# Grouping the attention products of a chunk by kind: all four pairs of heads at once

## The chip, the cores and the metric

The kernel runs on one core of a Trainium2 chip. The metric is the device time of one execution in microseconds. Before the change three runs took 1051.94, 1056.81 and 1057.1 us, with a median of 1056.81.

## The reference

A gated linear attention (4 sequences, 8 heads, 768 tokens, head size 48) is followed by two MLPs over 3072 tokens of 384 columns:

```python
for t in range(S):
    state = alpha[:, :, t, :, None] * state + einsum('bhd,bhde' outer product of k[t], v[t])
    y[:, :, t] = einsum('bhd,bhde->bhe', q[:, :, t], state)
...
h = x @ w_in;   x1 = (h * sigmoid(h)) @ w_out                    # 384 -> 2048 -> 384
out = (silu(x1 @ w_gate) * (x1 @ w_val)) @ w_out2                # 384 -> 1536 -> 384
```

## The kernel before

**Attention.** The tokens of a sequence are cut into 6 chunks of 128; with 4 sequences these are 24 chunks, ordered by chunk and then by sequence, so that chunk n has position c = n // 4 in sequence b = n % 4. The 8 heads are 4 pairs, the two heads of a pair on partitions 0 to 47 and 64 to 111. For each pair g (96 in all) the kernel makes keys times the decays behind them and queries over these (`stage_a1` to `stage_a3`: scans on VectorE, products on POOL and at the start on VectorE). `qkt(g)` makes the scores of both heads on TensorE and moves the keys to tokens on partitions; `causal(g)` masks the scores on VectorE into a tile `pt`; `keys(g)` copies the keys on ScalarE into a tile `kt`.

`pv(g)` is what the change touches. On TensorE it issues for one pair up to three kinds of plain float32 products, each once per head:

- the value product (L449), into the results `y`: 128 tokens deep, 64 columns wide, 128 moving columns. In the first four chunks a second product (L451) adds the values of pair 0 under the other pairs;
- the state product (L456), for c > 0, adds onto `y`: 64 rows deep, 48 wide, 128 moving columns;
- the increment product (L465), for c < 5, into `ds`: 128 deep, 64 wide, 48 moving columns.

The head decides which half of the columns of the array a product uses, and for the state product which half of the rows too. In the trace every float32 product appears as two matmul records, each with a weight load. `chunk_end(n)` copies a finished chunk's `y` out on ScalarE, with the difference to the full float32 on VectorE, and adds `ds` to the state.

**First MLP.** 24 chunks are 7 blocks of 4, 3, 3, 3, 3, 4, 4. For a block, 16 steps each take 9 products `g1` (L559 to L562) and 9 products `g2` (L594 to L597), 512 or 384 columns wide. Its weights come as 64-bit words that VectorE decodes (L47 to L57), during the first block only. **Second MLP.** 6 blocks of 12 steps, `gv` and `og`.

**The order** is written out by hand; every engine works its instructions in the order in which the program issues them. The first four chunks are attention alone: `attn(2)` issues one pair's products with a lag of two pairs, and then the next pair's scores. From then on, each step of the first MLP has two slots, one behind `g1` and one behind `g2`, and `slot` calls `attn` with lag 1: products of the oldest pair, then scores of a new pair if one is due (12 or 16 pairs over 24 of a block's 32 slots). The attention of a block is worked on in the slots of the block before it.

Of the kernel before, what the change touches and what calls it, by code (L numbers as in the profile page):

```python
# [21 lines left out]
C = 128  # L22
# [7 lines left out]
# Columns of the packed attention input: the decays of each pair of heads with a 0 before and behind  # L30
# them, then keys, queries and values.
# [4 lines left out]
# Bounds on the sums of squares of a chunk's scaled keys and queries, and on the squares of the sums  # L36
# of its results, which are finite with them.
# [3 lines left out]
def decode(eng, raw, tmp, step):  # L41
    """One of three steps from float64 words ([128, 2 n] int32) to the float32 with the same leading
    24 bits, in the place of the high words; the last returns those."""
# [20 lines left out]
def general(tc, pk, w1, w2, out):  # L64
    """The same function for inputs outside the range of the chunked form: the recurrence step by
    step over the tokens (a scan per value column), and the two MLPs in plain float32 products."""
# [154 lines left out]
def fast(ctx, tc, pk, w1, w2, out, bad_i):  # L221
    """Chunked attention in division form and both MLPs, float32 products as three float32r passes
    of operands that are split exactly into two parts."""
# [32 lines left out]
    # ---------------------------------------------------------------- attention  # L256
# [10 lines left out]
    # The keys of a pair with tokens on partitions, the columns of its heads at 0 and 64.  # L267
    kts = [ac.tile([128, 2, 64], F32, name=f"kt{i}") for i in range(3)]

    # Held for the first block of tokens only.  # L270
# [33 lines left out]
    # The score operands are made for two pairs of heads at a time.  # L304
# [7 lines left out]
    # Keys times the decays behind them, queries over these, in three steps. A scan starts anew with  # L312
    # data1 where its factor is 0, between the pairs.
# [11 lines left out]
    def stage_a2(d):  # L325
        n, ps_, _ = duo(d)
        kq_t[d] = ap.tile([128, 2, 2, C], F32, tag="kq", name=f"kq{d}", bufs=4)
        DVE.reciprocal(out=rc_t[d % 2][:, :, 0], in_=r_t[d][:, :, 0])
        KF(d).tensor_tensor(
            out=kq_t[d][:, 0], in0=in_t[n][1][:, 0, ps_], in1=r_t[d][:, :, 1:], op=ALU.mult  # L330
        )
# [40 lines left out]
    def guard(d):  # L372
        """Sums of squares that say at the end whether every product was in range."""
# [9 lines left out]
    def qkt(g):  # L383
        """Scores [key, query] of both heads of a pair, and the keys with tokens on partitions."""
# [3 lines left out]
        if n < NE:  # L388
            # Before the first MLP there is room for a bank per head.
# [15 lines left out]
    def causal(g):  # L405
        if g < NE * NP and g % NP == 0:
            pt = p0[g // NP % 2]
        else:
            pt = ap.tile([128, 2, C], F32, tag="pt", name=f"pt{g}", bufs=3)
# [11 lines left out]
    def keys(g):  # L421
        s = s_t.pop(g)[1]
        if g < (NCH - B) * NP:
            kt_t[g] = kts[g % 3].rearrange("p h x -> p (h x)")
            ACT.activation(
                out=kts[g % 3][:, :, :D], in_=s[:, :2 * D].rearrange("p (h d) -> p h d", h=2),
# [3 lines left out]
    def pv(g):  # L430
        n, p = divmod(g, NP)
        c, b = divmod(n, B)
        v = v_t[n]
        if p == 0:
            early = n % 2 if n < NE else 0
            y_t[n] = bank((6, 2)[early], f"y{n}")
            if c < NC - 1:
                ds_t[n] = bank((7, 3)[early], f"ds{n}")[:, :NP * D].rearrange(
                    "p (r e) -> p r e", r=NP
                )  # L440
        y = y_t[n]
        cs = slice(p * C, p * C + C)
        pt = pt_t.pop(g)
        if n < NE and p == 0:
            p0_t[n] = pt
        else:
            for h in range(2):
                hs = slice(64 * h, 64 * h + 64)
# [544 lines left out]
```

## Time and profile before

| | |
|---|---|
| runs | 1051.94, 1056.81, 1057.1 us |
| profiled execution, span from first to last instruction | 1050.7 us |
| TensorE, matmul | 1017.4 us busy (97%) |
| VectorE | 480.3 us (46%) |
| ScalarE | 366.1 us (35%) |
| POOL | 233.3 us (22%) |

The profiled execution is known by its span; the time around it is in the runs alone. PE is TensorE's matmuls, PEld its weight loads, DVE is VectorE, ACT is ScalarE. PEclk is the granted clock as a share of 2.4 GHz, so 0.5 is the lower level of 1.2 GHz. In a timeline a row merges equal instructions that follow each other (x4): its start is the first one's, its length runs to the end of the last one. Rows of matmuls overlap, since a row lasts until its results are written; the distance between two starts is what a matmul takes from the engine.

### The profile page before, as it was taken

How to read it: one execution, taken by the hardware profiler on the slowest of the kernel's cores; microseconds unless marked ns; L12 is line 12 of the kernel's file. 1: busy time of each engine (PE TensorE's matmuls, PEld its weight loads, DVE VectorE, ACT ScalarE, POOL GpSimd, SP SyncE). 2: the span in 40 equal slices, each digit the busy share in tenths (PEclk: the TensorE clock that was granted, in tenths of full speed). 3: DMA queues.
4: the chain of work that ended last, by engine and by line, in shares of the span. 5: the costliest groups of instructions: out<-in, count | busy, mean ns of one | idle time of the engine just before them, and what ended most of it. 6: DMA issues, size and time to landing. Idle time of an engine off the chain costs nothing.

```text
span 1050.7 us, 14356 instructions
## 1 busy us (share of the span) xinstructions
PE 1017.4 (97%) x5600; PEld 857.1 (82%) x5600; DVE 480.3 (46%) x869; ACT 366.1 (35%) x874; POOL 233.3 (22%) x303
## 2 busy tenths in 40 slices
PE   8888899999999999999999899999999999999997
PEld 5766688898988988877786688888888888888886
DVE  6999954434344354343279983223222222222222
ACT  2444444534444444444344432212212222222211
POOL 5566633313223233231024430000000000000000
PEclk8799999999999999999999999999999999999999
DMA  6544312121112122200155630100100100100000
GB/s 200 207 180 161 116 52 72 51 65 51 52 64 71 48 78 71 78 21 1 36 179 161 187 114 1 61 1 1 61 1 1 61 1 1 61 1 1 31 1 33
DMA packets 27883, 69.09 MB, mean 66 GB/s; under 512 B 3104, under 2 KB 9248, under 8 KB 27808
## 3 DMA queue, kind: packets, MB, share of 16 engines
q1 hardware_dynamic: 27808, 68.10, 20.1%
q8 instruction: 46, 0.75, 0.3%
q14 instruction: 29, 0.24, 0.1%
HBM read 56.68 MB, written 9.44 MB: 63 GB/s over the span
## 4 chain that ended last, share of the span: by engine, by line
PE 79%; DVE 12%; issue 5%; DMA 2%; POOL 1%; ACT 0%; SPq 0%; POOLq 0%; ACTq 0%; DVEq 0%
PE gv L560 9%; PE gv L559 9%; PE gv L562 9%; PE h L559 5%; PE o L664 5%; PE o L662 5%; PE o L663 5%; PE x L594 5%; PE x L595 5%; PE h L560 4%; PE h L562 4%; PE x L597 4%; DVE raw L52 3%; PE y L449 3%; DVE dec L47 2%
## 5 line engine op out<-in xcount | busy, mean ns | idle before, releaser
L560 PE MATMUL gv<-x1h,w 128*128 128x512 f32 x432 | 169.1, 391 | 0.0
L559 PE MATMUL gv<-x1h,w 128*128 128x512 f32 x432 | 169.0, 391 | 0.0
L647 DVE TENSOR_TENSOR a<-gv,sg 128x512 f32<-128x512 f32 x72 | 49.7, 690 | 259.9 <-PE gv L562 258.8
L559 PE MATMUL h<-x,w 128*128 128x384 f32 (+2 forms) x342 | 129.6, 379 | 0.6 <-ACT x L488 0.6
L594 PE MATMUL x<-gh,w 128*128 128x384 f32 (+1 forms) x336 | 122.7, 365 | 4.0 <-ACT gh L578 3.3
L560 PE MATMUL h<-x,w 128*128 128x384 f32 (+2 forms) x342 | 123.2, 361 | 0.0
L562 PE MATMUL gv<-x1l,w 128*128 128x512 f32 x432 | 122.1, 391 | 0.0
L595 PE MATMUL x<-gh,w 128*128 128x384 f32 (+1 forms) x336 | 121.2, 361 | 0.0
L578 ACT ACTIVATE gh<-h 128x384 fp32r<-128x384 f32 (+1 forms) x112 | 59.7, 533 | 167.6 <-PE h L562 167.5
L250 DVE TENSOR_TENSOR gl<-gf,gh 128x384 fp32r<-128x384 f32 (+1 forms) x112 | 72.4, 646 | 80.2 <-ACT gf L579 78.5
L645 ACT ACTIVATE sg<-gv 128x512 f32<-128x512 f32 x72 | 42.9, 596 | 173.3 <-PE gv L562 173.3
L253 ACT ACTIVATE ah<-a 128x512 fp32r<-128x512 f32 x72 | 45.5, 632 | 154.5 <-DVE a L647 154.5
L662 PE MATMUL o<-w,ah 128*128 128x384 f32 x288 | 97.1, 337 | 1.1 <-ACT ah L253 1.1
L664 PE MATMUL o<-w,al 128*128 128x384 f32 x288 | 97.3, 338 | 0.1
L663 PE MATMUL o<-w,ah 128*128 128x384 f32 x288 | 96.7, 336 | 0.0
L250 POOL TENSOR_TENSOR w<-raw,w 128x384 fp32r<-128x384 f32 x64 | 77.6, 1219 | 82.2 <-ACT w L536 78.9
L562 PEld LDWEIGHTS gv<-x1l,w 128*128 128x128 f32 x432 | 81.1, 188 | 17.8
L559 PEld LDWEIGHTS gv<-x1h,w 128*128 128x128 f32 x432 | 81.0, 188 | 15.3
L560 PEld LDWEIGHTS gv<-x1h,w 128*128 128x128 f32 x432 | 81.1, 188 | 15.0
L413 DVE TENSOR_TENSOR pt<-s,mask 128x256 f32<-128x256 f32 x80 | 33.8, 423 | 122.6 <-PE s L402 122.6
L597 PE MATMUL x<-gl,w 128*128 128x384 f32 (+1 forms) x336 | 85.7, 362 | 2.8 <-DVE gl L250 2.5
L562 PE MATMUL h<-x,w 128*128 128x384 f32 (+2 forms) x342 | 85.8, 359 | 0.0
(105 smaller groups left out, 1642.2 us busy)
## 6 DMA issues: line engine op xcount, KB each, us to landing
raw<-in_w_dram SPq DMA_DIRECT2D x64, 384.0 KB, 4.3
in<-in_pk_dram SPq DMA_DIRECT2D x23, 770.5 KB, 4.3
in_v<-in_pk_dram SPq DMA_DIRECT2D x24, 256.0 KB, 3.1
x1r<-x_d SPq DMA_DIRECT2D x6, 768.0 KB, 5.2
out_dram<-ob SPq DMA_DIRECT2D x24, 192.0 KB, 2.0
x_d<-x1e SPq DMA_DIRECT2D x3, 768.0 KB, 4.4
x_d<-x1e SPq DMA_DIRECT2D x4, 576.0 KB, 3.3
late<-in_w_dram SPq DMA_DIRECT2D x4, 384.0 KB, 5.1
```

The source lines that it names most:

```text
L250: eng.tensor_tensor(out=lo, in0=src, in1=hi.bitcast(F32), op=ALU.subtract)
L559: PE.matmul(acc, part(u, k), xh, start=(k == 0), stop=False)
L560: PE.matmul(acc, part(u, k, 1), xh, start=False, stop=False)
L562: PE.matmul(acc, part(u, k), xl, start=False, stop=(k == len(xk) - 1))
L578: ACT.activation(out=gh, in_=hb, func=AF.Silu)
L594: PE.matmul(x1_t[j][m], part(u, m), gh, start=(f == 0), stop=False)
L595: PE.matmul(x1_t[j][m], part(u, m, 1), gh, start=False, stop=False)
L597: PE.matmul(x1_t[j][m], part(u, m), gl, start=False, stop=(f == NF1 - 1))
L647: DVE.tensor_tensor(out=a, in0=val, in1=sg, op=ALU.mult)
L662: PE.matmul(o, ah[:, ts], ohl[:, :DM], start=(f == 0), stop=False)
L663: PE.matmul(o, ah[:, ts], ohl[:, DM:], start=False, stop=False)
L664: PE.matmul(o, al[:, ts], ohl[:, :DM], start=False, stop=(f == NF2 - 1))
```

## The change

`pv` takes a chunk instead of a pair. It issues the value products of all four pairs and both heads, then the increment products of all, then the state products of all. `attn` calls it when all four pairs of a chunk have their scores (and, with lag 2, one pair more); the three other calls of a chunk issue no products. Only the first value product of a chunk starts a new sum in the bank of `y`; the others write into the same bank without a start. To hold four pairs until then, there are 6 buffers of scaled keys and queries instead of 4, 5 masked score tiles instead of 3 and 5 key tiles instead of 3. The reserve for descriptors of dynamic DMAs is set to 4096 bytes. Comments are removed, which moves line numbers by a few (L449 becomes L445, L451 L450, L465 L459, L456 L467).

```diff
-    kts = [ac.tile([128, 2, 64], F32, name=f"kt{i}") for i in range(3)]
+    kts = [ac.tile([128, 2, 64], F32, name=f"kt{i}") for i in range(NP + 1)]
...
-        kq_t[d] = ap.tile([128, 2, 2, C], F32, tag="kq", name=f"kq{d}", bufs=4)
+        kq_t[d] = ap.tile([128, 2, 2, C], F32, tag="kq", name=f"kq{d}", bufs=6)
...
-            pt = ap.tile([128, 2, C], F32, tag="pt", name=f"pt{g}", bufs=3)
+            pt = ap.tile([128, 2, C], F32, tag="pt", name=f"pt{g}", bufs=NP + 1)
...
+    def pv(n):
         c, b = divmod(n, B)
         v = v_t[n]
+        early = n % 2 if n < NE else 0
+        y = y_t[n] = bank((6, 2)[early], f"y{n}")
+        first, last = n * NP, n * NP + NP
+        heads = [(p, h, slice(64 * h, 64 * h + 64)) for p in range(NP) for h in range(2)]
+        pts = [pt_t.pop(g) for g in range(first, last)]
+        for p, h, hs in heads:
+            if n < NE and p == 0:
+                continue
+            cs = slice(p * C, p * C + C)
+            PE.matmul(
+                y[hs, cs], v[:, p, hs], pts[p][:, h], start=(p == (n < NE)),
+                stop=(n >= NE and c == 0 and p == NP - 1),
+            )
+            if n < NE:
                 PE.matmul(
+                    y[hs, cs], v3[n % 2][:, p - 1, hs], pts[0][:, h], start=False,
+                    stop=(p == NP - 1),
                 )
         if c < NC - 1:
+            ds = ds_t[n] = bank((7, 3)[early], f"ds{n}")[:, :NP * D].rearrange(
+                "p (r e) -> p r e", r=NP
+            )
+            for p, h, hs in heads:
+                PE.matmul(
+                    ds[hs, p], kt_t[first + p][:, hs], v[:, p, 64 * h:64 * h + D],
+                    start=True, stop=True,
+                )
...
+        if c:
+            for p, h, hs in heads:
+                PE.matmul(
+                    y[64 * h:64 * h + D, p * C:p * C + C], state[b][hs, p],
+                    kq_t[(first + p) // 2][hs, 1, p % 2], start=False, stop=(p == NP - 1),
+                )
...
-        if st["qk"] - st["pv"] >= lag or not more:
-            if st["pv"] < st["qk"]:
-                pv(st["pv"])
-                st["pv"] += 1
+        if st["qk"] - st["pv"] * NP >= NP + lag - 1:
+            pv(done)
+            st["pv"] += 1
...
-        if st["pv"] > done and done % NP == NP - 1:
-            chunk_end(done // NP)
+        if st["pv"] > done:
+            chunk_end(done)
```

**Order, TensorE, in the slots of the first MLP.** Before, one slot behind `g2` (`x`) with the products of one pair, here the first pair of a chunk of the last sequence (`state_95`), and then the next `g1` (`h`); x2 is both heads:

```order
L597 MATMUL x_1_2_1591<-gl_0_1539,w_1_427 128x384
L449 MATMUL y_1601<-pt_1576,in_v_1166 64x128 x2
L456 MATMUL y_1601<-kq_1069,state_95 48x128 x2
L465 MATMUL ds_1602<-in_v_1166,kt_97 64x48 x2
L559 MATMUL h_2_1609<-x_888,w_4_594 128x384
```

After the change, the slot three steps on, behind the scores of the fourth pair of the same chunk:

```order
L602 MATMUL x_1_2_1595<-gl_3_1664,w_7_694 128x384
L445 MATMUL y_1730<-pt_1580,in_v_1170 64x128 x2
L445 MATMUL y_1730<-pt_1624,in_v_1170 64x128 x2
L445 MATMUL y_1730<-pt_1667,in_v_1170 64x128 x2
L445 MATMUL y_1730<-pt_1708,in_v_1170 64x128 x2
L459 MATMUL ds_1739<-in_v_1170,kt_99 64x48 x2
L459 MATMUL ds_1739<-in_v_1170,kt_100 64x48 x2
L459 MATMUL ds_1739<-in_v_1170,kt_96 64x48 x2
L459 MATMUL ds_1739<-in_v_1170,kt_97 64x48 x2
L467 MATMUL y_1730<-kq_1059,state_95 48x128 x4
L467 MATMUL y_1730<-kq_1210,state_95 48x128 x4
L564 MATMUL h_5_1765<-x_892,w_10_790 128x384
```

The products of three earlier slots have moved into this one, and the state products have moved behind the increments.

**Order, TensorE, in the first four chunks.** Before, around the last products of chunk 1: scores (`s`) of the ninth pair, products of the eighth, scores of the tenth:

```order
L393 MATMUL s_0_337<-kq_258 128x128
L393 MATMUL s_1_338<-kq_258 128x128
L394 MATMUL s_0_337<-start,kq_258 128x96
L449 MATMUL y_286<-pt_315,in_v_111 64x128
L451 MATMUL y_286<-start 64x128
L449 MATMUL y_286<-pt_315,in_v_111 64x128
L451 MATMUL y_286<-start 64x128
L465 MATMUL ds_287<-in_v_111,kt_97 64x48 x2
L393 MATMUL s_5_359<-kq_258 128x128
```

After, the end of the group of chunk 1 and the scores of the tenth pair (four rows each of the two pairs before, between the ninth pair's scores and these, are left out here):

```order
L445 MATMUL y_341<-pt_309,in_v_113 64x128
L450 MATMUL y_341<-start 64x128
L445 MATMUL y_341<-pt_309,in_v_113 64x128
L450 MATMUL y_341<-start 64x128
L459 MATMUL ds_354<-in_v_113,kt_100 64x48 x2
L459 MATMUL ds_354<-in_v_113,kt_96 64x48 x2
L459 MATMUL ds_354<-in_v_113,kt_97 64x48 x2
L459 MATMUL ds_354<-in_v_113,kt_98 64x48 x2
L393 MATMUL s_5_363<-kq_246 128x128
```

Between these two pairs' scores now stands the whole group of the chunk, where the products of one pair stood.

**Order, VectorE, at the end of the first four chunks.** Before, with `x` the eviction of chunk 3 and `raw`, `dec` the decoding of weights:

```order
L47 TENSOR_SCALAR dec_4_536<-raw_4_327 128x384
L250 TENSOR_TENSOR ql<-kq_448,qh 64x2x128
L52 SCALAR_TENSOR_TENSOR raw_4_327<-raw_4_327,dec_4_536 128x384
L47 TENSOR_SCALAR dec_5_560<-raw_5_423 128x384
L57 SCALAR_TENSOR_TENSOR raw_4_327<-raw_4_327 128x384
L250 TENSOR_TENSOR x_276<-y_483,x_276 128x3x128
```

After:

```order
L47 TENSOR_SCALAR dec_4_530<-raw_4_321 128x384
L250 TENSOR_TENSOR ql<-kq_436,qh 64x2x128
L250 TENSOR_TENSOR x_280<-y_546,x_280 128x3x128
L52 SCALAR_TENSOR_TENSOR raw_4_321<-raw_4_321,dec_4_530 128x384
L47 TENSOR_SCALAR dec_5_575<-raw_5_417 128x384
L57 SCALAR_TENSOR_TENSOR raw_4_321<-raw_4_321 128x384
```

The eviction stands three instructions earlier. This is the only difference on VectorE; ScalarE's order is the same, POOL gains two memsets of `kt` at the start, and on SP one load of values stands three weight loads earlier.

## Rows read from the trace of the kernel before

**Rows 1.** The page's totals: busy us, share of the span, instructions.

```profile
PE 1017.4 (97%) x5600; PEld 857.1 (82%) x5600; DVE 480.3 (46%) x869; ACT 366.1 (35%) x874; POOL 233.3 (22%) x303
```

**Rows 2.** Busy us (and instructions) of PE, PEld, DVE, ACT and POOL in stretches of the span, then the granted clock, the DMA share and GB/s.

```profile
0.00:48.00 48.00, 40.40 (x287) 30.15 (x288) 37.52 (x91) 16.93 (x57) 25.82 (x45) 0.79 0.57 189
48.00:134.00 86.00, 71.68 (x406) 52.99 (x406) 83.91 (x132) 39.87 (x102) 57.11 (x56) 0.98 0.45 158
134.00:506.00 372.00, 372.00 (x2401) 315.19 (x2400) 154.06 (x336) 165.91 (x463) 108.10 (x167) 1.00 0.18 55
```

**Rows 3.** Who waited for whom: us in total, times, longest us. The first row is of TensorE from 60 to 505 us, the second of VectorE from 10 to 60 us.

```profile
PE y L449 <- DVE pt L413: 10.7, 10, 1.7
...
DVE pt L419 <- PE s L394: 2.0, 2, 1.0
```

**Rows 4.** Busy us and records of PE and PEld in one stretch, of one line alone: first the state product (L456), then the increment product (L465; its PE count holds two records of another group, its count of weight loads does not).

```profile
134.00:506.00 372.00, 28.71 (x272) 11.38 (x272) 1.00 0.18 55
...
134.00:506.00 372.00, 16.80 (x210) 10.28 (x208) 1.00 0.18 55
```

**Rows 5.** Timeline of TensorE: start us, length us, engine, line, operation, tiles. First a slot of a middle chunk with a pair's products, then, behind the dots, one of a last chunk.

```profile
300.89 0.34 PE L595 MATMUL x<-gh,w 128*128 128x384 f32 x1
...
301.76 0.69 PE L597 MATMUL x<-gl,w 128*128 128x384 f32 x3
302.38 0.44 PE L449 MATMUL y<-pt,in_v 128*64 128x128 f32 x4
302.75 0.42 PE L456 MATMUL y<-kq,state 64*48 64x128 f32 x4
303.10 0.32 PE L465 MATMUL ds<-in_v,kt 128*64 128x48 f32 x4
303.35 0.44 PE L559 MATMUL h<-x,w 128*128 128x384 f32 x1
303.63 0.34 PE L560 MATMUL h<-x,w 128*128 128x384 f32 x1
...
441.26 0.40 PE L560 MATMUL h<-x,w 128*128 128x512 f32 x1
...
442.42 0.86 PE L562 MATMUL h<-x,w 128*128 128x512 f32 x3
...
444.27 0.40 PE L595 MATMUL x<-gh,w 128*128 128x512 f32 x1
```

**Rows 6.** The same view, a pair of an early chunk, where a second value product (L451) follows the first.

```profile
44.02 0.45 PE L449 MATMUL y<-pt,in_v 128*64 128x128 f32 x4
44.29 0.40 PE L451 MATMUL y<-start 128*64 128x128 f32 x4
44.51 0.28 PE L465 MATMUL ds<-in_v,kt 128*64 128x48 f32 x4
44.72 0.44 PE L559 MATMUL h<-x,w 128*128 128x384 f32 x1
```

**Rows 7.** The same view cut to short windows inside the value products of rows 5: weight loads that had begun by 302.50 us, and matmuls that had begun by 302.53 us.

```profile
302.38 0.20 PEld L449 LDWEIGHTS y<-pt,in_v 128*64 128x64 f32 x4 [0.25 <-issue]
...
302.38 0.33 PE L449 MATMUL y<-pt,in_v 128*64 128x128 f32 x2
```

**Rows 8.** Timeline around 133 us, the last pair of chunk 6: VectorE's masking, then TensorE. In brackets the idle time before a row and who ended it.

```profile
132.53 0.42 DVE L413 TENSOR_TENSOR pt<-s,mask 128x256 f32<-128x256 f32 x1
...
133.00 0.44 PE L449 MATMUL y<-pt,in_v 128*64 128x128 f32 x4 [1.03 <-DVE pt L413]
...
133.98 0.50 PE L559 MATMUL h<-x,w 128*128 128x512 f32 x1
```

**Rows 9.** Timelines of the first chunks: POOL's first product behind its memsets, its product for the ninth pair's queries, then TensorE and VectorE at the tenth pair, and TensorE at the lower clock; last, the stretch from 30 to 44 us as in rows 2.

```profile
7.04 0.68 POOL L329 TENSOR_TENSOR kq<-in,r 128x256 f32<-128x256 f32 x1 [1.82 <-DVE r L318]
...
21.64 0.98 POOL L342 TENSOR_TENSOR kq<-in,g 128x256 f32<-128x256 f32 x1 [2.87 <-DVE g L337]
...
24.78 0.49 PE L393 MATMUL s<-kq 64*128 64x128 f32 x4
25.20 0.46 PE L394 MATMUL s<-start,kq 128*128 128x96 f32 x2
...
26.96 0.47 DVE L419 TENSOR_TENSOR pt<-s,mask 128x128 f32<-128x128 f32 x2
...
30.82 0.89 PE L449 MATMUL y<-pt,in_v 128*64 128x128 f32 x4 [1.77 <-DVE pt L419]
31.30 0.83 PE L451 MATMUL y<-start 128*64 128x128 f32 x4
31.73 0.59 PE L465 MATMUL ds<-in_v,kt 128*64 128x48 f32 x4
32.25 0.80 PE L393 MATMUL s<-kq 64*128 64x128 f32 x4
...
30.00:44.00 14.00, 13.07 (x73) 10.81 (x73) 13.25 (x27) 5.07 (x17) 8.68 (x11) 0.51 0.47 162
```

**Rows 10.** Timeline around 301 us: VectorE's masking and its difference, and the product that reads the difference.

```profile
300.92 0.43 DVE L413 TENSOR_TENSOR pt<-s,mask 128x256 f32<-128x256 f32 x1 [3.13 <-PE s L402]
301.38 0.56 DVE L250 TENSOR_TENSOR gl<-gf,gh 128x384 fp32r<-128x384 f32 x1
...
306.53 0.68 PE L597 MATMUL x<-gl,w 128*128 128x384 f32 x3
```

More of the change, by code (lines that the diff above doesn't have):

```diff
@@ L423, in keys @@
         if g < (NCH - B) * NP:
-            kt_t[g] = kts[g % 3].rearrange("p h x -> p (h x)")
+            kt_t[g] = kts[g % (NP + 1)].rearrange("p h x -> p (h x)")
             ACT.activation(
-                out=kts[g % 3][:, :, :D], in_=s[:, :2 * D].rearrange("p (h d) -> p h d", h=2),
+                out=kts[g % (NP + 1)][:, :, :D], in_=s[:, :2 * D].rearrange("p (h d) -> p h d", h=2),
                 func=AF.Copy,
             )
-    def pv(g):
-        n, p = divmod(g, NP)
+    def pv(n):
@@ L432, in pv @@
         c, b = divmod(n, B)
         v = v_t[n]
[L434 to L448, printed above, removed]
-                PE.matmul(y[hs, cs], v[:, p, hs], pt[:, h], start=True, stop=(n >= NE and c == 0))
-                if n < NE:
-                    PE.matmul(
-                        y[hs, cs], v3[n % 2][:, p - 1, hs], p0_t[n][:, h], start=False, stop=True
-                    )
@@ L454, in pv @@
-        if c:
-            for h in range(2):
+        early = n % 2 if n < NE else 0
[12 more added lines that the diff above has]
+            if n < NE:
@@ L456, in pv @@
                 PE.matmul(
-                    y[64 * h:64 * h + D, cs], state[b][64 * h:64 * h + 64, p],
-                    kq_t[g // 2][64 * h:64 * h + 64, 1, g % 2], start=False, stop=True,
+                    y[hs, cs], v3[n % 2][:, p - 1, hs], pts[0][:, h], start=False,
+                    stop=(p == NP - 1),
                 )
         if c < NC - 1:
-            kt = kt_t.pop(g)
-            for h in range(2):
-                hs = slice(64 * h, 64 * h + 64)
-                es = slice(64 * h, 64 * h + D)
-                PE.matmul(ds_t[n][hs, p], kt[:, hs], v[:, p, es], start=True, stop=True)
+            ds = ds_t[n] = bank((7, 3)[early], f"ds{n}")[:, :NP * D].rearrange(
+                "p (r e) -> p r e", r=NP
+            )
@@ new lines, in pv @@
+            for p, h, hs in heads:
[3 more added lines that the diff above has]
+                )
+            for g in range(first, last):
+                kt_t.pop(g)
+        if c:
[4 more added lines that the diff above has]
+                )
@@ L977 @@
     from concourse.bass_utils import run_bass_kernel_spmd
-    nc = bacc.Bacc("TRN2", target_bir_lowering=False, num_devices=1)
+    nc = bacc.Bacc(
+        "TRN2", target_bir_lowering=False, num_devices=1, dynamic_dma_scratch_size=4096
+    )
     arrays, args = {}, []
```

## The prediction

> **What bounds the kernel now.** I read first the page's totals, then the busy time of each engine by stretch, then the waits, and last single slots in the timeline. TensorE is busy 97% of the span, but the stretches show that this average hides three parts [rows 1, 2]. From 0 to 48 us no engine is full: TensorE has 40.40 us and VectorE 37.52, with two waits of about 1.0 us for scores [rows 3]. From 48 to 134 us VectorE is the bound: 83.91 of 86 us busy with weight decoding and scans, while TensorE has 71.68 and waits for it: all ten waits of the value products for masked scores in the attention stretch, 10.7 us, go to this engine [rows 3], and the last one stands just before 133.00 us [rows 8]. From 134 to 506 us TensorE is busy 372.00 of 372 us, VectorE 154.06 and ScalarE 165.91: here, and only here, TensorE time is time of the kernel. After 506 us no attention product is left.
>
> So the question is what the changed products cost TensorE between 134 and 506 us. The counts by line give the amount: 272 records of the state product at 16 for each chunk (4 pairs, 2 heads, 2 records for each float32 product) are 17 chunks, and 208 weight loads of the increment product are 13 chunks [rows 4]. The other four of the 17 are the last chunk of each sequence, which makes no increment. Chunks 4 to 6 are worked on before 134 us, chunks 0 to 3 before 48 us.
>
> **What a pair costs today.** In the timeline of one slot, from the first L597 at 301.76 to the second product of the next group at 303.63 are 1.87 us [rows 5]. Four steps of plain products at 0.174 us (300.89 to 301.76 is five of them) would be 0.70 us. The pair's three kinds therefore cost 1.17 us: 0.10 before L449 starts (301.76 + 3 x 0.174 = 302.28, it starts at 302.38), 0.97 for the three kinds (0.37, 0.35, 0.25), and 0.11 because L559 takes 0.28 to its successor where 0.17 is usual. A chunk pays this four times: 4.69 us. For a chunk without increments, from 442.42 to 444.27 are 1.85 us less four steps of 0.232 (441.26 to 442.42 is five), so 0.92 us, and 3.68 a chunk [rows 5].
>
> What of this is streaming? The early chunks have a place where a second product of the same tile shape follows: L451 behind L449, then L465 behind L451 [rows 6]. There L449 takes 0.27 to its successor, not 0.37, L451 takes 0.22, and L465 with the end of the group 0.21. So 0.22 is the price of two passes of 128 columns for both heads side by side; the first load adds 0.05; and leaving the shape adds 0.10 (0.37 - 0.27). That a load of the next pass runs under the pass before is seen directly: by 302.50 all four loads of the pair had begun, while by 302.53 only two matmuls had [rows 7].
>
> **The change part by part.**
> - *Value products, four pairs in a row:* 0.27 + 3 x 0.22 = 0.93 us. They are followed by increments in the same tile shape, so no 0.10 is paid between them.
> - *Increments:* the first three pairs 0.21 - 0.10 = 0.11 each, the last 0.21 with the way out: 0.54 us.
> - *State products:* their shape (64 rows) never follows itself beyond one pair in this trace. Bounds: 0.22 a pair, as L451 streams the same 128 columns, or 0.35, what a pair costs alone. I take 0.22, since 0.35 holds a first load and a way out, which cannot recur inside a group: 0.35 + 3 x 0.22 = 1.01 us.
> - *Way in and out:* 0.10 and 0.11, once. A chunk costs 0.10 + 0.93 + 0.54 + 1.01 + 0.11 = 2.69 us, so 4.69 - 2.69 = 2.00 us less. Without increments: 0.10 + 0.93 + 0.10 + 1.01 + 0.11 = 2.25, 1.43 less. Sum between 134 and 506 us: 13 x 2.00 + 4 x 1.43 = **31.7 us less**.
> - *Moved work:* in the order shown for the TensorE-bound part, the products of the first three pairs leave their slots and stand with the fourth; the end of a chunk stays in the same slot, so the evictions, state sums and loads behind it hold their places. ScalarE's order does not change, POOL gains two small memsets ahead of its first product, before which it now sits idle for 1.82 us until VectorE is done [rows 9], and that idle time covers them; on SP one load of values moves ahead of three weight loads, which feeds a chunk two further on and costs nothing while VectorE sets the pace.
> - *Hand-over at 133 us:* the last pair of chunk 6 waits for its masked scores (done near 132.95), then takes 0.97 to the next product [rows 8]. In the change the first three pairs' values run under that wait, but the fourth pair's values (0.22 + 0.05), 0.54 of increments and 1.01 of states come behind it: 1.8 us, **0.8 us more**.
> - *The first 48 us:* no product with a state here, but the whole group of a chunk stands between two score products that VectorE reads. For chunk 1 it is 0.27 + 5 x 0.22 + 0.54 = 1.9 us where one pair's 0.70 stands today (44.02 to 44.72 [rows 6]). The scores before it need keys and queries that POOL finishes at 22.62, so they may start near 22.7; with 0.88 for them (24.78 to 25.66), 1.9 and 0.88 again, the next are ready at 26.4, before VectorE's 26.96 [rows 9]. At the lower clock (0.51 from 30 to 44 us, so nearly all at 1.2 GHz) a pair took 0.48 + 0.43 + 0.52 rather than 0.27 + 0.22 + 0.21; the group is then 0.48 + 5 x 0.43 + 3 x 0.22 + 0.52 = 3.8 us and the scores 1.4, and VectorE would wait 2.3 us. Chunk 0 wins up to 1.3 us (one of the waits for scores of about 1.0 goes [rows 3], and up to 0.3 with it) and gives it back behind its group, and some 2 us more at the lower clock. Bounds -1.3 to +4.5 (2.3 + 2.2); I take **0.5 us more**, near the case of the rows at the full clock. The eviction of chunk 3 moves ahead of a decode on VectorE, as the order shows; its products end near 45.6 in the new order and ScalarE's copy near 46.2, when VectorE comes free at 46.1, so it costs 0.1.
> - *Deeper buffers (masked scores, keys, scaled keys and queries):* they only loosen waits; a missing one would show as POOL or ScalarE waiting for TensorE.
>
> What is late next? A slot without products is 1.17 us shorter. The chain that a slot needs: VectorE's difference ends at 301.94, and the L597 that reads it starts at 306.53 [rows 10]. 4.6 us of room less 1.2 leaves 3.4, so nothing new ends last.
>
> Sum: 31.7 - 0.8 - 0.5 = 30.4 us off. The page gives the profiled execution's span, 1050.7 us, and not what lies around it; the three runs lie 1.2 to 6.4 us above the span, their median 1056.81 being 6.1 above. Span after: 1020.3 us; time, with the same 6.1: **1026.4 us**.
>
> **The rivals.**
> 1. *Loads exposed inside a group.* If a load waits for the pass that streams, seven more passes of each kind pay 0.05: 3 x 7 x 0.05 = 1.05 us a chunk, 0.70 without increments, 16.5 us in all; the time would be 1043 us. If only the first load of each further pair did, it would be 3 x 3 x 0.05 = 0.45, 7 us in all, and 1033.4 us. Against it stand the loads that begin under a pass and the 0.22 of L451 [rows 6, 7]; for it, that the 64-row shape is seen only for one pair. This is also what the Trainium skill would make of it ("TensorE: Matmul & The Clock Gate", Part 3, The mechanism): a weight load overlaps with a matmul in flight only when its row group differs, and here every pair of a head has the same row group. The trace disagrees for the value shape, where the loads of the second passes begin before the first have ended [rows 7]. Chance 0.08.
> 2. *The array empties between pairs all the same.* Then only three ways in and out a chunk go: 3 x 0.21 x 17 = 10.7, less 1.3: 1047.4 us. Nothing in rows 6 speaks for it. Chance 0.04.
> 3. *The room is taken up by another wait* (the one score bank, which masking and key copies must free before the next pair). Where two slots in turn make scores, 1.17 us of products no longer stand between them. If all of it came back, no change: 1056 us. Against it: masking takes 0.43 us and begins right behind the scores [rows 10]. Chance 0.03.
> 4. *Slower: the two heads lose their side-by-side run* in a long group, because one head's passes queue behind the other's. Then 8 more passes of each kind: 8 x (0.11 + 0.055 + 0.11) = 2.2 us a chunk, 1.76 without increments: 35.6 us, against 31.7 won, with 0.8 and 0.5, and some 3 us in the early groups: 1065 us. It decides from the point where nine tenths of the passes are no longer side by side. Against it: in rows 6 four passes a head run in pairs of heads. Chance 0.03.
>
> **How the numbers follow.** The forecast has 0.82, with its own range of 1019 to 1034 us: the early bounds, half the state's bounds (0.13 x 3 x 17 = 6.6 us) and the 5 us by which the three runs differ. The range of 1017 to 1043 us takes in the first rival and leaves out some 0.16. About 0.5% is what a measurement of this kernel can tell from no change. Faster by more than that, under 1051.5: 0.93, the forecast and the rivals 1 and 2 at nearly full weight; within it 0.04; slower 0.03.
>
> **What would show it.** After the change, between the end of VectorE's bound and the last attention product, TensorE should still be busy throughout, over some 340 us rather than 372. In one group there, 16 value records should take 0.93 us to the first increment, the increments 0.54 to the first state, and the states 1.01 to the next product. State records at 0.30 a pair or more would say rival 1; gaps of 0.10 between pairs, rival 2; a head's records behind the other's, rival 4. VectorE should leave its bound within a few us of 134. I am wrong if TensorE waits there for anything for more than 2 us in all, or if VectorE's part grows by over 5 us.

## The result, and the profile after

| | before | after |
|---|---|---|
| median (runs) | 1056.51 us (4) | 1025.14 us (4) |
| lowest to highest | 1051.94 to 1057.10 | 1024.40 to 1026.05 |
| span of the profiled execution | 1050.7 us | 1022.7 us |

The ratio is 0.9716, with a 95% interval of 0.9693 to 0.9738: the change makes the kernel 31.4 us faster by the medians. The forecast was 1026.4 us, within 1017 to 1043. The runs of the kernel before spread over 5 us, and its profiled execution is one of the shorter ones, so the two spans lie closer together than the medians.

The page's totals of the changed kernel, as [rows 1]:

```profile
PE 978.4 (96%) x5600; PEld 859.7 (84%) x5600; DVE 481.7 (47%) x869; ACT 367.8 (36%) x874; POOL 236.2 (23%) x305
```

The number of matmuls and of weight loads is the same, 5600. TensorE is busy 39 us less, and the span is only 28.0 us shorter: the share of TensorE that waits has grown a little. Where, the stretches show (columns as in [rows 2]; the first three stretches are the early part, VectorE's part and the part that TensorE fills, the last three are cuts around its start):

```profile
0.00:48.00 48.00, 35.35 (x287) 27.20 (x288) 36.49 (x89) 16.85 (x57) 25.44 (x47) 0.86 0.56 186
48.00:134.00 86.00, 66.38 (x372) 52.01 (x370) 83.87 (x132) 38.90 (x98) 57.28 (x56) 0.96 0.45 160
136.50:476.80 340.30, 340.30 (x2399) 319.13 (x2397) 154.12 (x333) 165.57 (x457) 109.72 (x165) 1.00 0.20 60
...
130.00:134.00 4.00, 1.05 (x15) 0.68 (x14) 3.97 (x7) 1.59 (x4) 2.29 (x2) 1.00 0.00 0
134.00:136.00 2.00, 2.00 (x34) 1.93 (x36) 1.97 (x4) 1.98 (x7) 0.82 (x1) 0.74 0.12 11
136.00:138.00 2.00, 2.00 (x10) 1.35 (x7) 1.50 (x3) 1.14 (x4) 2.00 (x4) 0.50 0.38 124
```

Before 134 us TensorE saves 10.4 us (40.40 + 71.68 less 35.35 and 66.38; part of it is the clock, 0.86 in the first 48 us against 0.79), but VectorE is as busy there as before, 83.87 of 86 us against 83.91, so nothing comes of that. From 136.5 us on TensorE is busy in all of 340.30 us, and every microsecond saved there counts.

One chunk's group in that part, in the timeline of TensorE (columns as in [rows 5]); behind the dots a chunk of the last four, which makes no increments:

```profile
311.93 1.09 PE L445 MATMUL y<-pt,in_v 128*64 128x128 f32 x16
312.85 0.62 PE L459 MATMUL ds<-in_v,kt 128*64 128x48 f32 x16
313.40 1.08 PE L467 MATMUL y<-kq,state 64*48 64x128 f32 x16
314.41 0.45 PE L564 MATMUL h<-x,w 128*128 128x384 f32 x1
314.69 0.34 PE L565 MATMUL h<-x,w 128*128 128x384 f32 x1
...
458.67 1.09 PE L445 MATMUL y<-pt,in_v 128*64 128x128 f32 x16
459.69 1.08 PE L467 MATMUL y<-kq,state 64*48 64x128 f32 x16
460.70 0.50 PE L564 MATMUL h<-x,w 128*128 128x512 f32 x1
```

A row now holds 16 records where [rows 5] has 4. The distances between starts are 0.92 us for the values, 0.55 for the increments and 1.01 for the states: 2.48 us from the first value to the next plain product, where four pairs took 4 x 0.97 = 3.88. The plain product behind still takes 0.28 to its successor instead of 0.17, but once a chunk and not four times. In the last chunks, 458.67 to 460.70 is 2.03 us.

Now the hand-over from VectorE's part to TensorE's, as [rows 8] (VectorE's masking first, then TensorE):

```profile
130.13 0.88 PE L445 MATMUL y<-pt,in_v 128*64 128x128 f32 x12
...
133.48 0.42 DVE L413 TENSOR_TENSOR pt<-s,mask 128x256 f32<-128x256 f32 x1
...
133.96 0.44 PE L445 MATMUL y<-pt,in_v 128*64 128x128 f32 x4 [2.95 <-DVE pt L413]
134.22 0.62 PE L459 MATMUL ds<-in_v,kt 128*64 128x48 f32 x16
134.78 1.82 PE L467 MATMUL y<-kq,state 64*48 64x128 f32 x16
136.53 0.79 PE L564 MATMUL h<-x,w 128*128 128x512 f32 x1
...
138.62 0.40 PE L565 MATMUL h<-x,w 128*128 128x512 f32 x1
```

The three pairs that are ready run ahead, and then TensorE stands still for 2.95 us in one piece, where single slots used to wait about 1 us each. Behind that pause the clock is not the full one: 0.74 between 134 and 136 us, and 0.50, the level of 1.2 GHz, between 136 and 138 (cut finer, it is 1.00 up to 134.94 and 0.50 from there to 138.36). So the states take 1.75 us instead of 1.01, and the first five plain products 2.09 (136.53 to 138.62) instead of five times 0.232, which is 1.16.

Who waited for whom: first TensorE from 40 to 478 us, then, behind the dots, VectorE from 10 to 60 us (as [rows 3]):

```profile
PE y L445 <- DVE pt L413: 8.8, 3, 3.0
PE h L565 <- POOL w L250: 7.2, 5, 1.9
...
DVE pt L419 <- PE s L394: 3.5, 1, 3.5
```

Ten waits of 10.7 us have become three of 8.8: gathered as the products are. The five waits for weights from POOL, 7.2 us, are new; they lie before the hand-over, where VectorE sets the pace. On VectorE two waits for scores of 2.0 us in all (and one of 0.3, for the first pair of a chunk) have become one of 3.5, behind the group of chunk 0.

### The profile page after: what moved, and what is told of

Read it like the earlier page. It is cut to its first block, busy times and chain, and to the rows that moved or that the text cites. A ratio compares the mean times of both kernels' runs of the same rounds, so it can differ in the third digit from the quotient of the medians.

```text
span 1022.7 us, 14293 instructions
## 1 busy us (share of the span) xinstructions
PE 978.4 (96%) x5600; PEld 859.7 (84%) x5600; DVE 481.7 (47%) x869; ACT 367.8 (36%) x874; POOL 236.2 (23%) x305
## 4 chain that ended last, share of the span: by engine, by line
PE 79%; DVE 12%; issue 5%; DMA 2%; POOL 1%; ACT 1%; SPq 0%; POOLq 0%; DVEq 0%; ACTq 0%
PE gv L565 9%; PE gv L564 9%; PE gv L567 9%; PE h L564 5%; PE o L669 5%; PE o L667 5%; PE o L668 5%; PE h L565 5%; PE x L600 5%; PE x L599 5%; PE h L567 5%; PE x L602 5%; DVE raw L52 3%; DVE dec L47 2%; DVE raw L57 2%
## 5 line engine op out<-in xcount | busy, mean ns | idle before, releaser
L565 PEld LDWEIGHTS h<-x,w 128*128 128x128 f32 x342 | 65.4, 191 | 14.5 <-POOL w L250 9.4
```

What stands on the lines that cost most here:

```text
L565: PE.matmul(acc, part(u, k, 1), xh, start=False, stop=False)
```

## The experiments

In every comparison the kernel before ran on the same chip in the same session; its medians there were 1054.72, 1055.79 and 1056.24 us. Experiments 1, 2 and 4 and the first kernel of 3 are of the first session, 5, 6 and the other two kernels of 3 of the second, 7 of the third, and the change itself was measured ahead of them. Where two variants of different sessions are set beside each other and differ by a few us, their profiles have to agree with it.

**1. Is it the grouping, or the single visit?** All four pairs in one slot, but pair by pair inside it, each with its three kinds in the order of before.

```diff
...
+        for q in range(NP):
             for p, h, hs in heads:
+                if p != q or (n < NE and p == 0):
+                    continue
...
+            if c:
+                for p, h, hs in heads:
+                    if p == q:
...
+            if c < NC - 1:
+                for p, h, hs in heads:
+                    if p == q:
...
```

> All four pairs of a chunk are issued in one slot as in the change, but pair by pair (values, states, increments), so the kinds are not grouped. Theory (shape changes: each kind pays a first load of 0.05 us and a way out of 0.10 us, only where TensorE is the bound): only three ways in and out of 0.21 us a chunk are saved, 17 x 0.63 = 10.7 us of the kernel before, less 3 to 5 us that the late group costs around 134 us and in the first chunks; 1046 to 1052 us, 21 to 27 us slower than the change. Rival (the gain comes from one visit a chunk instead of four, or from the deeper buffers): within 4 us of the change, 1021 to 1029 us. In the trace the theory wants a chunk's group at 4 x 0.97 = 3.9 us from its first product to the next plain product, the rival near 2.5.

Measured: 1041.0 us (1039.85 to 1041.36), ratio 0.9867 (0.9845 to 0.989). Its timeline of TensorE, the first pair of a chunk, the start of the second, and the end:

```profile
300.59 0.44 PE L450 MATMUL y<-pt,in_v 128*64 128x128 f32 x4
300.96 0.42 PE L458 MATMUL y<-kq,state 64*48 64x128 f32 x4
301.31 0.32 PE L465 MATMUL ds<-in_v,kt 128*64 128x48 f32 x4
301.46 0.40 PE L450 MATMUL y<-pt,in_v 128*64 128x128 f32 x4
...
303.82 0.32 PE L465 MATMUL ds<-in_v,kt 128*64 128x48 f32 x4
304.07 0.44 PE L564 MATMUL h<-x,w 128*128 128x384 f32 x1
```

The group takes 3.48 us (300.59 to 304.07), exactly a microsecond more than in the change, and 13 x 1.0 + 4 x 0.85 = 16.4 us account for the 15.9 measured (0.85 is the 2.88 of a group in its last chunks less 2.03). So the single visit (in which increments and values now stand next to each other) is worth about half, and the grouping by kind the other half. It came out below the expected figure because I overlooked that an increment and the next pair's value share a tile shape: the increment takes 0.15 to its successor here and 0.25 at the end, so in the three places where a pair's increments are followed by the next pair's values nothing is paid for a change of shape.

Its hand-over shows one thing more. TensorE waits there for 1.11 us in one piece, hardly longer than the 1.03 of the kernel before [rows 8], and yet the clock behind it is at 0.50, as it is behind the 2.95 of the change (the last pair's values, then the stretch as in [rows 2]):

```profile
134.57 0.44 PE L450 MATMUL y<-pt,in_v 128*64 128x128 f32 x4 [1.11 <-DVE pt L413]
...
135.75:139.16 3.41, 3.41 (x9) 2.63 (x9) 2.94 (x7) 2.56 (x9) 3.36 (x4) 0.50 0.23 77
```

So the length of this one pause does not settle by itself whether the clock falls.

**2. The order of the kinds.** States between values and increments: the same products, but one change of shape more in a chunk.

```diff
...
+        if c:
+            for p, h, hs in heads:
+                PE.matmul(
+                    y[64 * h:64 * h + D, p * C:p * C + C], state[b][hs, p],
...
         if c < NC - 1:
             ds = ds_t[n] = bank((7, 3)[early], f"ds{n}")[:, :NP * D].rearrange(
...
-        if c:
-            for p, h, hs in heads:
...
```

> The change with the states issued between values and increments, the kinds still grouped. Theory (shape changes): one more of them in each chunk with increments, 0.10 for the way out of the values and 0.05 for the increments' first load: the group is 2.63 us rather than 2.48, and the kernel 13 x 0.15 = 2 us slower than the change, 1027 us. Rival (the number of groups counts, not the shapes that follow each other): the same group of 2.48 us, 1025 us.

Measured: 1029.88 us (1028.46 to 1030.55), ratio 0.9763 (0.974 to 0.9786).

```profile
298.62 1.09 PE L445 MATMUL y<-pt,in_v 128*64 128x128 f32 x16
299.64 1.08 PE L456 MATMUL y<-kq,state 64*48 64x128 f32 x16
300.65 0.67 PE L465 MATMUL ds<-in_v,kt 128*64 128x48 f32 x16
301.25 0.44 PE L564 MATMUL h<-x,w 128*128 128x384 f32 x1
```

The group is 2.63 us, 0.15 more than 2.48: the values now take 0.10 to leave their shape (1.02 to their successor, not 0.92), and the increments 0.05 for their first load (0.60, not 0.55). That is 2.0 us in 13 chunks, as expected (the whole stretch from the eleventh plain product behind the hand-over to the end of attention is 1.6 us longer than in the change, 338.6 against 337.0). The other 2.7 us by which the medians differ do not lie there: in its profile the last mask of VectorE's part stands at 136.28 instead of 133.48 us, after 5.8 us of waits for scores, with a mean clock of 0.79 in the first 48 us against 0.86. The order of the first four chunks, which have no states, is the same as in the change; why all four runs took longer was not settled.

**3. The hand-over and the early chunks.** Three kernels keep the pairs of before, slot by slot, for some chunks and group the rest. In the first these are chunks 0 to 6, as shown; the second has `done < 4 * NP` there, and the third `NE * NP <= done < 7 * NP`, which is chunks 4 to 6:

```diff
...
-        if st["qk"] - st["pv"] * NP >= NP + lag - 1:
-            pv(done)
-            st["pv"] += 1
+        if done < 7 * NP:
+            if (st["qk"] - done >= lag or not more) and done < st["qk"]:
+                pv_pair(done)
+                st["pv"] += 1
+        elif st["qk"] - done >= NP + lag - 1:
+            pv(done // NP)
+            st["pv"] += NP
...
```

> Chunks 0 to 6 pair by pair as in the kernel before, grouped by kind from chunk 7 on, the buffers as in the change. Theory (grouping pays only where TensorE is the bound, and costs before that: VectorE waits 3.5 us for scores behind chunk 0's group, and at 131 us TensorE waits 2.95 us in one piece and then runs 3 us at the lower clock): it gets all of the gain and none of the cost; the first TensorE-bound product comes 3.3 us earlier than in the change, 1021 to 1022.5 us. Rival (the early part does not count, or grouping helps there too): 1025 us or more.

> The first four chunks pair by pair, chunks 4 to 6 grouped as in the change. Against the run that groups from chunk 7, only chunks 4 to 6 differ. Theory (a group that must wait for its last masked scores idles TensorE in one piece and then runs at the lower clock, and the last of these groups, at about 135 us, is on the path): 2 to 3 us slower than grouping from 7, 1025.5 to 1026.5 us, with the last group before 140 us at 2.4 to 2.8 us behind its masks. Rival (chunks 4 to 6 lie behind VectorE and count for nothing): 1023.5 us.

> The first four chunks grouped as in the change, chunks 4 to 6 pair by pair, grouped from 7. Theory: it keeps what grouping does for the first 48 us (the run with pairs there had its last mask at 135.63 us, the change at 133.48, with the clock low for longer) and drops the wait and the low clock at 131 to 138 us, 2.4 us: 1022 to 1023 us, faster than the change and at least as fast as grouping from 7. Rival (the first 48 us differ by chance alone): 1023.5 us, as grouping from 7.

Together with the change they make a table of four (medians, us):

| | chunks 4 to 6 in pairs | chunks 4 to 6 grouped |
|---|---|---|
| chunks 0 to 3 in pairs | 1023.49 | 1025.56 |
| chunks 0 to 3 grouped | 1022.86 | 1025.14 |

The lowest and highest runs are 1022.43 and 1023.67, 1023.68 and 1026.65 in the first line, 1022.16 and 1024.71, 1024.40 and 1026.05 in the second. Read by line: grouping chunks 4 to 6 costs 2.1 or 2.3 us, twice the same. Read by column: grouping chunks 0 to 3 costs nothing that the medians show (0.4 or 0.6 us less, inside the spread). The first kernel came out above the 1021 to 1022.5 us that were expected: in its profile the mean clock of the first 48 us is 0.61, against 0.86 in the change, and the last mask stands at 135.63 us, 2.15 later. The other two lie in their ranges. The four medians are of three sessions, so the hand-over itself is the better witness of what chunks 4 to 6 do, and it agrees. The kernel with groups from chunk 7 on has the short hand-over of before:

```profile
136.10 0.44 PE L491 MATMUL y<-pt,in_v 128*64 128x128 f32 x4 [1.04 <-DVE pt L413]
...
137.07 0.50 PE L601 MATMUL h<-x,w 128*128 128x512 f32 x1
```

The one with groups from chunk 4 on has the long one of the change, 2.95 us of waiting and 2.52 to the next plain product:

```profile
133.99 0.44 PE L445 MATMUL y<-pt,in_v 128*64 128x128 f32 x4 [2.95 <-DVE pt L413]
...
136.51 0.80 PE L601 MATMUL h<-x,w 128*128 128x512 f32 x1
```

**4. The deeper buffers alone**, with the smaller reserve for descriptors and the pairs of before.

```diff
...
-    kts = [ac.tile([128, 2, 64], F32, name=f"kt{i}") for i in range(3)]
+    kts = [ac.tile([128, 2, 64], F32, name=f"kt{i}") for i in range(NP + 1)]
...
-        kq_t[d] = ap.tile([128, 2, 2, C], F32, tag="kq", name=f"kq{d}", bufs=4)
+        kq_t[d] = ap.tile([128, 2, 2, C], F32, tag="kq", name=f"kq{d}", bufs=6)
...
-            pt = ap.tile([128, 2, C], F32, tag="pt", name=f"pt{g}", bufs=3)
+            pt = ap.tile([128, 2, C], F32, tag="pt", name=f"pt{g}", bufs=NP + 1)
...
```

> The kernel before with the change's buffers (6 of scaled keys and queries, 5 masked score tiles, 5 key tiles, the smaller reserve for descriptors) and its old order. Theory: nothing waits for a buffer, so 1056 us, no change. Rival (part of the gain is looser buffers or other places in memory): faster than the kernel before by 3 us or more.

Measured: 1056.54 us (1053.40 to 1056.97, ten runs), ratio 1.0015 (0.9999 to 1.0031): the buffers bring nothing by themselves. Its profiled execution took 1056.79 us and has a span of 1055.1, against the 1050.7 of the kernel before, so the two show how executions of one order differ. Stretches of the early part in this kernel:

```profile
12.00:20.00 8.00, 7.12 (x52) 6.06 (x52) 4.99 (x16) 2.22 (x8) 4.12 (x6) 0.50 0.50 177
20.00:30.00 10.00, 10.00 (x68) 7.89 (x66) 6.70 (x18) 2.91 (x11) 3.62 (x5) 0.50 0.49 170
```

and the same stretches of the kernel before:

```profile
12.00:20.00 8.00, 7.16 (x63) 5.97 (x64) 5.45 (x18) 2.57 (x10) 4.14 (x6) 0.71 0.48 169
20.00:30.00 10.00, 7.97 (x84) 6.25 (x84) 8.91 (x22) 4.54 (x17) 4.24 (x6) 1.00 0.74 272
```

The clock is at 0.50 in both stretches here, at 0.71 and then 1.00 there. At the lower level TensorE needs all of the 10 us for 68 records, where it does 84 in 7.97. The scores come late, and VectorE is busy 6.70 us instead of 8.91. Its waits for scores are 6.5 us in all against 2.3 (with those for the first pair of a chunk, 1.2 and 0.3), and the last mask of its part stands at 136.22 us against 132.53. These 3.7 us are most of the 4.4 between the two spans; the other 0.7 lie behind attention.

**5. Do the two heads need to alternate?** Rival 4 of the prediction, brought about by the order: within a group all pairs of the first head, and then all of the second.

```diff
-        heads = [(p, h, slice(64 * h, 64 * h + 64)) for p in range(NP) for h in range(2)]
+        heads = [(p, h, slice(64 * h, 64 * h + 64)) for h in range(2) for p in range(NP)]
```

> The change with each kind's products issued for all pairs of the first head, then for all pairs of the second. Theory A (each half of the array takes its own products from the queue as far as the queue looks ahead): a group of 2.48 us as before, 1025 us. Theory B (the look-ahead ends after a few products, so that the heads no longer run side by side): up to 8 x (0.11 + 0.058 + 0.11) = 2.2 us more a chunk, 1.8 without increments, so up to 36 us slower, 1061 us, and a group up to 4.7 us.

Measured: 1050.4 us (1046.41 to 1051.94), ratio 0.9951 (0.9923 to 0.9978): nearly all of the gain is gone. From a short window of its timeline, up to 0.45 us behind the first value, and then the end of the same group:

```profile
312.40 0.65 PE L445 MATMUL y<-pt,in_v 128*64 128x128 f32 x4
...
314.36 1.55 PE L467 MATMUL y<-kq,state 64*48 64x128 f32 x16
315.84 0.45 PE L564 MATMUL h<-x,w 128*128 128x384 f32 x1
```

The same window of the change, up to 0.45 us behind its first value at 311.93:

```profile
311.93 0.66 PE L445 MATMUL y<-pt,in_v 128*64 128x128 f32 x8
```

Four records have begun here, eight there: only one head is at work at first. At 312.89, when the fifth pass of the first head begins, another begins with it. The trace does not name the head, but passes of one head follow each other at 0.109 us, so it must be the first of the second head: the engine reached past the four passes that were left of one head, and not past the eight at the start. So on TensorE a product can begin ahead of one that was issued before it; that every engine works its instructions in the order of issue, as is said of the kernel before, does not hold there for the two halves of the array. The group takes 3.44 us (312.40 to 315.84), 0.96 more, or 16.3 us in 17 chunks. The other 9 us by which the medians differ lie before. In the profiled execution, which is 27.5 us longer than that of the change, the last mask stands at 142.54 us, 9.1 later, after 8.4 us of VectorE's waits for scores, and from the end of that mask to the eleventh plain product it takes 8.5 us instead of 5.9, the clock being at 0.50 from 144.4 us on.

**6. Half groups.** Two pairs at a time, in the same slot.

```diff
...
+        for part_ in (heads[:NP], heads[NP:]):
+            for p, h, hs in part_:
...
+            if c < NC - 1:
+                for p, h, hs in part_:
...
+            if c:
+                for p, h, hs in part_:
...
```

> The change with each chunk's group cut in two: kinds of pairs 0 and 1, then kinds of pairs 2 and 3. Theory (shape changes): two more a chunk, states to values and values or increments to states, each 0.10 for the way out and 0.04 to 0.05 for a first load, so 0.30 us more a chunk: group 2.78 instead of 2.48, without increments 2.32 instead of 2.03; 17 x 0.30 = 5 us slower, 1030 us. Rival (only one visit a chunk counts): 1025 us.

Measured: 1028.31 us (1027.63 to 1028.92), ratio 0.9747 (0.9727 to 0.9767).

```profile
296.08 0.66 PE L450 MATMUL y<-pt,in_v 128*64 128x128 f32 x8
296.57 0.39 PE L460 MATMUL ds<-in_v,kt 128*64 128x48 f32 x8
296.89 0.64 PE L466 MATMUL y<-kq,state 64*48 64x128 f32 x8
297.46 0.66 PE L450 MATMUL y<-pt,in_v 128*64 128x128 f32 x8
...
298.83 0.45 PE L565 MATMUL h<-x,w 128*128 128x384 f32 x1
```

The group is 2.75 us, 0.27 more than in the change for two more changes of shape; with 0.29 in the last four chunks that is 13 x 0.27 + 4 x 0.29 = 4.7 us. Measured were 3.2, between the medians and between the two profiled spans. In the profiles 4.3 us of it lie between the eleventh plain product behind the hand-over and the end of attention (341.3 against 337.0). At the hand-over half of the group is done ahead of the wait, and the next plain product starts at 135.49, not 136.53; but the clock is at 0.50 from 135.44 to 138.85, so that at the eleventh plain product only 0.3 us of the 1.0 is left (139.43 against 139.76). The other 0.8 lie behind attention (545.2 against 545.9).

**7. Is it the clock that spreads the early part?** Products that nobody reads (128 x 128 in bfloat16, one record each), into a bank that is free at that time, keep TensorE busy while it waits for POOL and ScalarE. First in the third kernel of experiment 3, with 44 ahead of the fourth pair's scores and 28 ahead of the ninth's; then in the kernel before, with 24 each ahead of the third and the fourth pair's.

```diff
...
+        if st["qk"] in (3, 8) and more:
...
+            for _ in range({3: 44, 8: 28}[st["qk"]]):
+                PE.matmul(fills[0][:, :C], mask, mask, start=True, stop=True)
...
```

> The kernel with pairs in chunks 4 to 6, and 44 and 28 small products that nobody reads in two places where TensorE waits: before the scores of pair 3 (idle 2.07 us there) and of pair 8 (idle 1.84 us). Theory (those waits let the clock fall to half, 0.50 from 12 to 20 and from 25 to 30 us in that run, and VectorE then waits 6.1 us for scores behind the two groups): the clock stays at 1.0 at least to 20 us, VectorE's waits for scores fall by 2 us or more in most executions, its last mask comes before 134 us, and the time is 1020 to 1021.5 us. Rival (the clock is not what VectorE waits for, or the fillers only delay the scores): 1023 us or more.

> The kernel before, with 24 such products before the scores of pair 2 and 24 before those of pair 3. Theory (the spread of the kernel before, 1051.6 to 1057.6 us, is the clock's luck in the first 48 us: its profile of 1050.7 us span has 1.0 from 18 to 30 us, that of the kernel with deeper buffers, 1055.1 us, stays at 0.50 from 12 to 40 us, and VectorE waits 6.5 us for scores there instead of 2.3): the clock is held more often, and the median comes down to 1052 to 1053 us. Rival (the spread has another cause, such as when transfers land): the median stays at 1055 to 1056 us.

Measured: the first 1020.3 us (1019.73 to 1021.75, five runs), ratio 0.9667 (0.9648 to 0.9686), the fastest of all and as expected; the second 1051.54 us (1050.40 to 1051.92, six runs), ratio 0.9958 (0.9942 to 0.9974), a little below the 1052 to 1053 expected. The early stretches of the first:

```profile
12.00:20.00 8.00, 6.59 (x81) 5.34 (x79) 5.71 (x20) 3.58 (x14) 4.15 (x6) 1.00 0.60 226
20.00:30.00 10.00, 6.82 (x91) 5.62 (x88) 9.37 (x25) 3.79 (x15) 4.74 (x7) 1.00 0.72 255
```

and of the kernel it was made from, in a profile of the longest of its four runs (1024.71 us):

```profile
12.00:20.00 8.00, 7.33 (x57) 6.19 (x57) 4.52 (x13) 2.22 (x8) 3.92 (x6) 0.50 0.75 269
20.00:30.00 10.00, 8.16 (x65) 6.80 (x65) 7.03 (x18) 2.91 (x11) 3.62 (x5) 0.67 0.44 143
```

With the fillers the clock is 1.00 in both, VectorE is busy 9.37 of 10 us, its waits for scores fall from 6.1 to 1.7 us, and the last mask stands at 132.10 us instead of 136.39. The 2.6 us between the medians (1022.86 and 1020.3) are of two sessions. The same stretches of the kernel before with fillers (those without stand in experiment 4):

```profile
12.00:20.00 8.00, 7.53 (x92) 6.23 (x89) 6.48 (x20) 3.73 (x14) 4.14 (x6) 1.00 0.54 197
20.00:30.00 10.00, 7.10 (x74) 5.53 (x74) 9.31 (x25) 3.64 (x14) 4.34 (x7) 1.00 0.79 283
```

Here too the clock is 1.00, VectorE's waits for scores are 0.8 us in all, and the last mask stands at 131.81 us. The six runs lie within 1.6 us (1050.40 to 1051.92), those without fillers in the same session within 5.8 (1052.04 to 1057.78). So the spread of the kernel before goes with the clock of the first 48 us: holding that up takes it away.

## Why the prediction was right

**The main term** stood: 31.7 us less were forecast between the hand-over and the last attention product, and 32.0 were measured (from the fifth plain product behind the hand-over to the end of attention, 370.4 us before and 338.4 after). Its pieces, 0.93 for the values, 0.54 for the increments and 1.01 for the states, measured 0.92, 0.55 and 1.01. The value that rows of before did not show, 0.22 for a further pair of states, was the right end of its bounds; had it been 0.35, the states would have taken 1.40.

**Rival 1** (exposed loads) and **rival 2** (an empty array between pairs) fall with these durations: there is no gap between the pairs of a kind. Rival 2's mechanism is real where shapes do change, as experiments 1, 2 and 6 show, at 0.15 us a change (0.10 to leave, 0.05 for the first load). **Rival 3** falls too, since TensorE waits for nothing between 136.5 and 476.8 us. **Rival 4** did not happen because heads alternate product by product; experiment 5 makes it happen at 0.96 us a chunk, not the 2.2 I put on it, since the second head starts behind four passes of the first and the two then run side by side.

**The hand-over** was mis-sized: 0.8 us forecast, 2.1 to 2.3 measured in experiment 3, and 2.4 in the two profiles (1.6 from the end of the mask to the next plain product, 2.63 against 1.03, and 0.8 on the products behind, those at the lower clock). What was missing is the clock: I had laid the group's parts behind the mask at the full one, and without the 0.74 by which the states took longer the 1.6 would be 0.9. I did not see that the waits of four slots would be gathered into one pause of 2.95 us, nor that the clock would be at 1.2 GHz behind it.

**The first 48 us:** 0.5 us more were taken within bounds of -1.3 to 4.5. In the profiles the last mask stands 0.95 later (133.48 against 132.53), but the table of experiment 3 shows no cost of grouping there. The prediction gave the lower clock a bound (VectorE waits 2.3 us), and one wait of 3.5 us came, behind chunk 0's group at that clock; but the same kernel varies by some 5 us in this part with the clock, more than the term. The range held these 5 us, without their cause.

**Deeper buffers at nothing:** right, by experiment 4. **The room for the next chain**, 3.4 us: right, TensorE waits for nothing between the hand-over and the end of attention.

**The sum against its own time** had a slip. I added 6.1 us around the span, the median less the span of the profiled execution. But a run's time is its span and 1.7 us (1024.4 and 1022.7 after), so the profiled execution of before had taken some 1052.4 us, and the other 4.4 go with the clock of the first 48 us, which differs from run to run (experiments 4 and 7). The change has not shown such a spread in its four runs.

So part of the closeness is luck. The span was forecast as 1020.3 us and came out as 1022.7, 2.4 longer: the 28.0 us between the two spans are the 32.0 of the main term, less 2.4 at the hand-over, less 0.95 by which the last mask is later, less 0.6 behind attention (545.9 against 545.3 us), where 30.4 were forecast. Around the span I added 6.1 us, and the median after lies 2.4 above it, 3.7 less. The two misses offset each other to 1.3 us. The main term owes nothing to this. The pair of kernels with the clock held up by fillers (each with its own) shows it most plainly: 1051.54 and 1020.3 us, 31.2 less, with chunks 4 to 6 in pairs. Their profiled spans, 1050.0 and 1018.7, differ by 31.3, which are 32.0 less 0.3 at the last mask (132.10 against 131.81) and 0.4 behind attention (545.8 against 545.4).

**Open:** why experiment 2 took longer in its early part in all four runs, what sets the clock there from one run to the next, and what makes it fall behind the hand-over.

## What to carry to other kernels

Small products of different tile shapes can cost more by their changes than by their columns (of the 1.17 us of a pair here, 0.55 were columns: 0.22, 0.22 and 0.11): gather them by shape, put kinds of equal shape next to each other, and keep the two halves of the array alternating product by product. Do it where TensorE is the bound, and not just ahead of that: there a group gathers the waits as well, and in this kernel the clock fell just when TensorE's time began to count, so that the last chunks before the hand-over were better left in small pieces. Where a part with idle TensorE leads into a chain that waits for it, some unread products in its pauses may be worth more than they cost.

## What was not expected of the hardware

- Leaving a tile shape costs 0.10 us and the first load in the next one 0.05, while in one shape 128 columns for both heads side by side cost 0.109 us a pass (0.22 a pair), 64 rows deep as well as 128, and 48 columns 0.058 (0.11 a pair, by the 0.39 and 0.62 of rows of 8 and 16).
- TensorE reached past about four passes that were left of one half of the array to start the other half, and not past eight (experiment 5).
- In the profiles of all six kernels that work chunk 6 in one slot (the change, experiments 1, 2, 5 and 6, and the second kernel of 3) the granted clock is at 0.50 for 3.4 us behind the hand-over (6.8 in experiment 5); their pauses there are 1.11 to 2.96 us. In those of the six that keep its pairs in four slots it stays at 1.00 from 130 to 146 us; their pauses are 0.97 to 1.04. What in the gathered order brings the clock down is not shown: 1.11 and 1.04 us lie close together.
- 72 unread products of 128 columns, in two rows of 2.62 and 1.73 us at the full clock, went with a kernel 2.6 us faster (1022.86 to 1020.3, in two sessions); 48 of them took 4.7 us off the kernel before (1056.24 to 1051.54, in one).
